# Seven block products for eight in the gate and value projections of the last two token blocks

## The chip, the cores and the metric

The kernel runs on one core of one Trainium2 chip. The metric is the device time of one execution in microseconds (us). The kernel before was timed in three runs; one more execution was profiled.

## The reference, cut to what matters

Attention over chunks of 32 tokens (each chunk sees 8 memory keys and 56 neighbours) gives `x` with 3072 rows of 512. Two feed-forward layers follow:

```python
gate = 1.0 / (1.0 + np.exp(-(x @ w_gate)))      # w_gate, w_val: 512 x 1536
x2 = (gate * (x @ w_val)) @ w_out               # w_out: 1536 x 512
h = x2 @ w_in                                   # w_in: 512 x 2048
P = a[0] + a[1] * h + a[2] * h**2 + a[3] * h**3
Q = 1.0 + np.abs(b[0]) * np.abs(h) + np.abs(b[1]) * h**2
y = (P / (Q + 1e-06)) @ w_out2                  # 2048 x 512
```

## The kernel before

The 3072 tokens are six blocks of 512. Every product of the two layers is three matmuls, since each operand is split into a rounded high part and the rest (`TERMS`: high by high, high by low, low by high). A matmul here multiplies a 128 x 128 weight tile by 512 tokens.

**First layer.** The loop over `steps` has 72 steps: for each block `j` the twelve slices `f` of 128 features. A step computes the gate (`gate_val` with m = 0: 4 slices of K times 3 terms, 12 matmuls), the value (m = 1, 12 more), their product `g` in two parts (`g_split`), and then the output product of the step before (`out1`, 12 matmuls into four accumulators that stay over the block). The weights stay in SBUF as 32-bit words (`wf`), and every step of every block splits its three weight tiles again: ScalarE writes the high part (`w1_hi`, line 323), VectorE the low part (`w1_lo`, line 327).

**Around it.** The attention of block `j` is done in pairs of 128 tokens during the steps of block `j - 1`, in three places of the PE order: scores (`pair_qk`), transposes (`pair_t`) and values (`pair_out`), put into a step by the table `plan`. The weights of the second layer arrive as 64-bit words, are converted (`conv2`), stored in DRAM as `w2d` and read again in block 5 and after, where they are split.

**Second layer.** 96 steps of `h2` (12 matmuls), the rational function on ScalarE and VectorE, and `out2` (12 matmuls) five steps later.

The order on every engine is the order of the code. Each engine runs its own list in that order, and so does SyncE (SP), which issues nearly all the transfers: one that waits for a buffer holds up all those behind it. Buffers come from pools: `w` (32 tiles of 4 KB a partition), `t` for intermediates, and PSUM with four banks `ps` beside the four accumulators.

Of the kernel before, what the change touches and what calls it, by code (L numbers as in the profile page):

```python
# [34 lines left out]
PAD = 840  # L35
# [3 lines left out]
NPAIR = 8  # L39


@with_exitstack
def fused_kernel(ctx: ExitStack, tc: tile.TileContext, q, k, v, w1, w2, coef, x2d, w2d, out):
# [16 lines left out]
    psp = ctx.enter_context(tc.tile_pool(name="ps", bufs=4, space=PSUM))  # L60

# [110 lines left out]
    def attn_pv(t, x, n0):  # L172
# [82 lines left out]
    def pair_pv(t, x, n0):  # L257
# [53 lines left out]
    def unit1(f, m):  # L311
        u = 3 * f + m
        if u % 2 == 0 and u // 2 not in wf:
            wf[u // 2] = wpool.tile([P, 2, 512], F32, tag="w", name=f"wf{u // 2}")
        return wf[u // 2][:, u % 2]

    def load_w1(f):
        for m in range(3):
            load_stage(f"1_{f}_{m}", w1[:, f, m * 512 : (m + 1) * 512])

    def split_hi(key, src):
        wp[key] = wpool.tile([P, 2, 512], F32R, tag="w", name="wp" + "_".join(map(str, key)))
        nc.scalar.activation(out=wp[key][:, 0], in_=src, func=ACTF.Copy)  # L323
# [4 lines left out]


# [3 lines left out]
    xt, gp, sgs = {}, {}, {}  # L333

    def gate_val(j, f, m, c0, n):
        w, x = wp[1, j, f, m], xt[j]
        pt = ps(f"h{j}_{f}_{m}_{c0}")[:, 0:n]
        for kt in range(KT):
            for i, (a, b) in enumerate(TERMS):
                nc.tensor.matmul(  # L340
                    pt,
                    lhsT=w[:, a, kt * P : (kt + 1) * P],
                    rhs=x[:, kt, b, c0 : c0 + n],
                    start=(kt == 0 and i == 0),
                    stop=(kt == KT - 1 and i == 2),
                )
        if m == 0:
            sgs[j, f, c0] = t2(f"sg{j}_{f}_{c0}")[:, 0:n]
            nc.scalar.activation(out=sgs[j, f, c0], in_=pt, func=ACTF.Sigmoid)  # L349
        else:  # L350
            sg = sgs[j, f, c0]
            nc.vector.tensor_tensor(out=sg, in0=sg, in1=pt, op=ALU.mult)  # L352
        if c0 + n == BLOCKS1[j]:
            del wp[1, j, f, m]
# [29 lines left out]

    def store1(j):
        for d in range(KT):
            s = t2(f"x2s{j}_{d}")
            if d % 2 and j < NB1 - 1:
                nc.vector.tensor_copy(s, acc[j][d])
            else:  # L390
                nc.scalar.activation(out=s, in_=acc[j][d], func=ACTF.Copy)
            nc.sync.dma_start(out=x2d[j, :, d], in_=s)
        del acc[j]


    x2f, x2, w2f, rat = {}, {}, {}, {}
# [5 lines left out]
    def split_x2(j, d):  # L402
        if d == 0:
            x2[j] = xpool.tile([P, KT, 2, 512], F32R, tag="x", name=f"x2_{j}")
        s, t = x2f.pop((j, d)), x2[j]
        nc.scalar.activation(out=t[:, d, 0], in_=s, func=ACTF.Copy)
        nc.vector.tensor_tensor(out=t[:, d, 1], in0=s, in1=t[:, d, 0].bitcast(F32), op=ALU.subtract)

    def load_w2(i):
        w2f[i] = t2(f"w2f{i}")  # L410
        nc.sync.dma_start(out=w2f[i], in_=w2d[i])

    def split_w2(i):
        s = w2f.pop(i)
        split_hi((2, i), s)
        split_lo((2, i), s)

    def h2(j, f):
# [3 lines left out]
        for kt in range(KT):  # L422
            for i, (a, b) in enumerate(TERMS):
# [3 lines left out]
                    rhs=x[:, kt, b],  # L427
# [59 lines left out]

    const.tile([P, PAD], F32, name="pad")


    NB1 = len(BLOCKS1)

    def pv(t):
        j, n0 = t // 4, t % 4 * P
        if n0 == 0:
            xt[j] = xpool.tile([P, KT, 2, 512], F32R, tag="x", name=f"x{j}")
        (attn_pv if t < NPAIR else pair_pv)(t, xt[j], n0)

# [294 lines left out]
```

## Time and profile before

| | |
|---|---|
| median of three runs | 1197.31 us (1196.38 to 1197.61) |
| the profiled execution | 1197.76 us; its span, first to last instruction, is 1196.0 us |
| PE (matmul) busy | 1183.2 us, 99% |
| PE weight loads busy | 975.4 us, 82% |
| VectorE (DVE) / ScalarE (ACT) busy | 842.0 us, 70% / 747.2 us, 62% |
| moved by DMA | 101.68 MB, 85 GB/s over the span |
| granted TensorE clock, mean | 0.993 of full speed (2.4 GHz) |

The profiled time is the span and 1.8 us around it. Busy shares are means over stages that have different limits.

### The profile page before, as it was taken

The numbers are of one execution on the slowest core, as the hardware profiler recorded it, in microseconds if no ns is written. First come the engines' busy times: TensorE is split into PE (matmuls) and PEld (weight loads), VectorE is DVE, ScalarE is ACT, GpSimd is POOL, SyncE is SP. The second block draws the span as 40 slices with busy tenths as digits, with TensorE's granted clock in tenths as the row PEclk, the third lists the DMA queues.
The fourth block names the chain that finished last, engine by engine and source line by source line (L and its number), as shares of the span: only waits on it lengthen the run. The fifth ranks groups of instructions, "written<-read, shape, count | busy, mean of one in ns | idle before, by whom it ended". The sixth has DMA issues, their size and how long they took to land.

```text
span 1196.0 us, 19841 instructions
## 1 busy us (share of the span) xinstructions
PE 1183.2 (99%) x8086; PEld 975.4 (82%) x8089; DVE 842.0 (70%) x1312; ACT 747.2 (62%) x1278; POOL 2.1 (0%) x15
## 2 busy tenths in 40 slices
PE   7999999999999999999999999999999999999998
PEld 4788888888888888888888888888888888888887
DVE  5777454555646454654566599898898898888885
ACT  5887445454546454554555687767776767776764
POOL 0000000000000000000000000000000000000000
PEclk8899999999999999999999999999999999999999
DMA  9854042234225224322532110100100100100000
GB/s 380 299 193 132 26 141 89 100 128 140 89 100 170 90 93 139 114 76 98 185 95 63 55 36 10 53 17 1 53 18 1 54 18 10 45 18 1 36 1 35
DMA packets 40123, 101.68 MB, mean 85 GB/s; under 512 B 4576, under 2 KB 4832, under 8 KB 40032
## 3 DMA queue, kind: packets, MB, share of 16 engines
q1 hardware_dynamic: 39456, 99.01, 24.6%
q8 instruction: 63, 1.03, 0.4%
q10 hardware_dynamic: 576, 1.41, 0.3%
q14 instruction: 28, 0.23, 0.1%
HBM read 79.43 MB, written 20.97 MB: 84 GB/s over the span
## 4 chain that ended last, share of the span: by engine, by line
PE 98%; DMA 1%; ACT 1%; issue 0%; DVE 0%; SPq 0%
PE h L340 33%; PE acc L463 22%; PE h L424 22%; PE acc L375 17%; PE xp L268 1%; PE sp L208 1%; PE xp L183 1%; DMA st<-w_in 1%; PE tp L253 1%; DMA q<-q_in 0%; PE tp L168 0%; PE sp L109 0%; ACT st L298 0%; ACT st L299 0%; ACT at L170 0%
## 5 line engine op out<-in xcount | busy, mean ns | idle before, releaser
L340 PE MATMUL h<-x,wp 128*128 128x512 f32 x1728 | 409.9, 392 | 1.5 <-ACT x L192 1.5
L340 PEld LDWEIGHTS h<-x,wp 128*128 128x128 f32 x1728 | 325.2, 189 | 69.2 <-ACT x L192 1.6
L424 PE MATMUL h<-x,wp 128*128 128x512 f32 x1152 | 276.5, 389 | 0.0
L463 PE MATMUL acc<-wp,g 128*128 128x512 f32 x1152 | 275.9, 389 | 0.0
L424 PEld LDWEIGHTS h<-x,wp 128*128 128x128 f32 x1152 | 216.2, 188 | 44.9
L463 PEld LDWEIGHTS acc<-wp,g 128*128 128x128 f32 x1152 | 216.2, 188 | 44.9
L375 PE MATMUL acc<-g,wp 128*128 128x512 f32 x864 | 212.8, 392 | 0.0
L375 PEld LDWEIGHTS acc<-g,wp 128*128 128x128 f32 x864 | 160.6, 188 | 34.0
L352 DVE TENSOR_TENSOR sg<-sg,h 128x512 f32<-128x512 f32 x72 | 49.5, 687 | 159.8 <-PE h L340 109.8
L432 ACT ACTIVATE t<-h,cf 128x512 f32<-128x512 f32 x96 | 74.6, 778 | 131.4 <-PE h L424 131.4
L358 ACT ACTIVATE g<-sg 128x512 fp32r<-128x512 f32 x72 | 45.4, 630 | 166.1 <-DVE sg L352 166.1
L327 DVE TENSOR_TENSOR wp<-wf,wp 128x512 fp32r<-128x512 f32 x216 | 136.6, 685 | 7.6 <-ACT wp L323 7.2
L323 ACT ACTIVATE wp<-wf 128x512 fp32r<-128x512 f32 x216 | 120.7, 621 | 10.2 <-PE h L340 8.8
L435 DVE TENSOR_TENSOR t<-t,h 128x512 f32<-128x512 f32 x96 | 65.8, 686 | 47.8 <-ACT hh L434 46.5
L349 ACT ACTIVATE sg<-h 128x512 f32<-128x512 f32 x72 | 43.0, 597 | 75.0 <-PE h L340 74.3
L359 DVE TENSOR_TENSOR g<-sg,g 128x512 fp32r<-128x512 f32 x72 | 49.9, 693 | 56.1 <-ACT g L358 56.1
L436 DVE SCALAR_TENSOR_TENSOR t<-t,cf,h 128x512 f32<-128x512 f32 x96 | 71.8, 748 | 3.4
L444 ACT ACTIVATE y<-qq,qc 128x512 f32<-128x512 f32 x96 | 70.0, 729 | 3.9 <-DVE qq L437 3.3
L437 DVE SCALAR_TENSOR_TENSOR qq<-hh,cab,qq 128x512 f32<-128x512 f32 x96 | 71.8, 748 | 0.0
L451 DVE SCALAR_TENSOR_TENSOR t<-t,cf,y 128x512 f32<-128x512 f32 x96 | 71.8, 748 | 0.0
L450 DVE SCALAR_TENSOR_TENSOR qq<-qq,y 128x512 f32<-128x512 f32 x96 | 66.0, 687 | 8.1 <-ACT y L445 8.1
L452 DVE SCALAR_TENSOR_TENSOR t<-qq,t 128x512 f32<-128x512 f32 x96 | 66.5, 692 | 3.3
(74 smaller groups left out, 833.2 us busy)
## 6 DMA issues: line engine op xcount, KB each, us to landing
st<-w_in SPq DMA_DIRECT2D x68, 512.0 KB, 4.7
v<-v_in SPq DMA_DIRECT2D x24, 512.0 KB, 4.7
k<-k_in SPq DMA_DIRECT2D x21, 416.0 KB, 4.0
w2d<-c SPq DMA_DIRECT2D x32, 256.0 KB, 2.1
w2f<-w2d SPq DMA_DIRECT2D x32, 256.0 KB, 3.4
q<-q_in SPq DMA_DIRECT2D x24, 256.0 KB, 3.6
x2d<-x2s SPq DMA_DIRECT2D x24, 256.0 KB, 2.8
x2f<-x2d SPq DMA_DIRECT2D x24, 256.0 KB, 3.1
```

The lines of the kernel that those rows point to most:

```text
L323: nc.scalar.activation(out=wp[key][:, 0], in_=src, func=ACTF.Copy)
L327: nc.vector.tensor_tensor(out=t[:, 1], in0=src, in1=t[:, 0].bitcast(F32), op=ALU.subtract)
L340: nc.tensor.matmul(pt, lhsT=w[:, a, kt * P : (kt + 1) * P], rhs=x[:, kt, b, c0 : c0 + n], start=(kt == 0 and i == 0), stop=(kt == KT - 1 a ...
L375: nc.tensor.matmul(acc[j][d][:, c0 : c0 + n], lhsT=w[:, a, d * P : (d + 1) * P], rhs=g[:, b, 0:n], start=(f == 0 and c0 == 0 and i == 0), ...
L424: nc.tensor.matmul(hp, lhsT=w[:, a, kt * P : (kt + 1) * P], rhs=x[:, kt, b], start=(kt == 0 and i == 0), stop=(kt == KT - 1 and i == 2),)
L432: nc.scalar.activation(out=t, in_=hp, func=ACTF.Identity, scale=cf[:, 3:4], bias=cf[:, 2:3])
L436: nc.vector.scalar_tensor_tensor(out=t, in0=t, scalar=cf[:, 1:2], in1=hp, op0=ALU.add, op1=ALU.mult)
L437: nc.vector.scalar_tensor_tensor(out=qq, in0=hh, scalar=cab[:, 1:2], in1=qq, op0=ALU.mult, op1=ALU.add)
L444: nc.scalar.activation(out=y, in_=qq, func=ACTF.Abs_reciprocal_sqrt, bias=qc[:, 0:1])
L451: nc.vector.scalar_tensor_tensor(out=t, in0=t, scalar=cf[:, 0:1], in1=y, op0=ALU.add, op1=ALU.mult)
L452: nc.vector.scalar_tensor_tensor(out=t, in0=qq, scalar=2.0, in1=t, op0=ALU.subtract, op1=ALU.mult)
L463: nc.tensor.matmul(acc[j][m], lhsT=g[:, a, m * P : (m + 1) * P], rhs=w[:, b], start=(f == 0 and i == 0), stop=(f == NF2 - 1 and i == 2),)
```

## The change

Blocks 4 and 5 (`JA`, `JB`) are no longer computed one after the other. Two blocks of tokens, two slices of features and two halves of K make a 2 x 2 x 2 block product, which the new function `quad` computes with seven products in place of eight. A product is 6 matmuls (two slices of K, three terms). `quad(fp, 0, ...)` makes the gates of features 2fp and 2fp + 1 for both blocks, `quad(fp, 1, ...)` the values; there are six `fp`. The seven products use sums and differences of the operands:

- of the weights: `w_comb` forms four per pair of features, one in each step of blocks 1 and 2, and stores them split (`wqs`);
- of x: `x_comb` forms five in steps 43 to 47, from x kept whole (`xf`);
- of the results: five additions in each `quad`.

So x of block 5 must be there before block 4 begins. The attention of blocks 2 to 5 is now done in the steps of blocks 1 to 3, one pair every three steps. A step exists only for blocks 0 to 3 (48 steps); after the last `quad` come 13 visits of `out1` alone.

SBUF would not hold all of this, so split weights are kept in DRAM: gate and value tiles are stored in block 1 and output tiles in block 2 (`wqa`), and blocks 3, 4 and 5 load them split instead of splitting them. The second layer's weights are stored split too. A split tile is 128 x 1024 words, 512 KB. Pools are opened and closed by stage; `w` has 18 buffers, `t` 14. The weight tiles of gate and value are laid out by halves of K, each with gate and value columns.

```diff
-    wpool = ctx.enter_context(tc.tile_pool(name="w", bufs=32))
-    xpool = ctx.enter_context(tc.tile_pool(name="x", bufs=2))
+    wpool = ctx.enter_context(tc.tile_pool(name="w", bufs=18))
+    xpool = ctx.enter_context(tc.tile_pool(name="x", bufs=4))
-    tpool = ctx.enter_context(tc.tile_pool(name="t", bufs=12))
+    tpool = ctx.enter_context(tc.tile_pool(name="t", bufs=14))
...
+    def load_qk2(t):
+        u = qs[t] = wpool.tile([P, 2, 4, P], F32, tag="w", name=f"q{t}")
+        nc.sync.dma_start(out=u, in_=q[t : t + 2].rearrange("t p r n -> p t r n"))
+        for i in range(2):
+            u = ks[t + i] = wpool.tile([P, KW], F32, tag="w", name=f"k{t + i}")
+            nc.sync.dma_start(out=u, in_=k[t + i])
...
+            c = slice(n0, n0 + 2 * P)
+            if j <= JA:
+                hi, lo = (xt[j][h][:, :, b, c] for b in range(2))
+                nc.scalar.activation(out=hi, in_=xps[h], func=ACTF.Copy)
+                nc.vector.tensor_tensor(out=lo, in0=xps[h], in1=hi.bitcast(F32), op=ALU.subtract)
+            if j >= JA:
+                nc.scalar.activation(out=xf[j][:, h, :, c], in_=xps[h], func=ACTF.Copy)
...
+    def store_split(key, dst):
+        nc.sync.dma_start(out=dst, in_=wp[key].bitcast(F32))
...
+    def load_split(key, src, p=None, tag="w"):
+        nc.sync.dma_start(out=split_tile(key, p, tag).bitcast(F32), in_=src)
...
+    def x_comb(o, c):
+        c = slice(256 * c, 256 * c + 256)
+        a, b = xf[JA], xf[JB]
+        key = f"{o}_{c.start}"
+        if o not in xop:
+            xop[o] = b_tile(f"b{o}", F32R, [P, 2, 2, 512])
+        if o == "22":
+            xs[key] = b[:, 1, :, c]
+            return
+        t = xs[key] = t2(f"xs{key}").rearrange("p (k n) -> p k n", k=2)
+        x0, x1 = {
+            "1": (b[:, 0, :, c], a[:, 0, :, c]),
+            "2": (b[:, 1, :, c], xs.get(f"1_{c.start}")),
+            "3": (b[:, 1, :, c], b[:, 0, :, c]),
+            "4": (a[:, 1, :, c], xs.get(f"2_{c.start}")),
+        }[o]
+        nc.vector.tensor_tensor(out=t, in0=x0, in1=x1, op=ALU.subtract)
...
+    def w_comb(i):
+        fp, o = divmod(i, 4)
+        a, b = wf["gv", 2 * fp], wf["gv", 2 * fp + 1]
+        sf[i] = t2(f"sf{i}")
+        x0, x1, op = (
+            lambda: (b[:, 0], b[:, 1], ALU.add),
+            lambda: (sf[i - 1], a[:, 0], ALU.subtract),
+            lambda: (a[:, 0], b[:, 0], ALU.subtract),
+            lambda: (a[:, 1], sf[i - 2], ALU.subtract),
+        )[o]()
+        nc.vector.tensor_tensor(out=sf[i], in0=x0, in1=x1, op=op)
...
+    PRODUCTS = (
+        (("a", 0, 0), "11", 0),
+        (("s", 1), "2", 1),
+        (("s", 0), "1", 2),
+        (("s", 2), "3", 3),
+        (("a", 0, 1), "21", 0),
+        (("s", 3), "22", 2),
+        (("a", 1, 1), "4", 3),
+    )
...
+    def quad(fp, m, fill):
+        f0, f1 = 2 * fp, 2 * fp + 1
+        bank = [ps(f"p{fp}_{m}_{i}") for i in range(4)]
+        def product(i):
+            w, o, n = PRODUCTS[i]
+            wt, x = wp[quad_key(fp, w)], xop[o]
+            for kt in range(2):
+                c = m * 256 + kt * P
+                for t, (a, b) in enumerate(TERMS):
+                    nc.tensor.matmul(
+                        bank[n],
+                        lhsT=wt[:, a, c : c + P],
+                        rhs=x[:, kt, b],
+                        start=(i < 4 and kt == 0 and t == 0),
+                        stop=(kt == 1 and t == 2),
+                        skip_group_check=True,
+                    )
+            if m == 1:
+                del wp[quad_key(fp, w)]
+                if i < len(PRODUCTS) - AHEAD and fp < NF1 // 2 - 1:
+                    quad_load(fp + 1, i + AHEAD, 1)
+        def add(out, x0, x1):
+            nc.vector.tensor_tensor(out=out, in0=x0, in1=x1, op=ALU.add)
+        def done(j, f, c):
+            if m == 0:
+                if c is None:
+                    sgs[j, f] = t2(f"sg{j}_{f}")
+                    nc.scalar.activation(out=sgs[j, f], in_=bank[0], func=ACTF.Sigmoid)
+                else:
+                    sgs[j, f] = c
+                    nc.scalar.activation(out=c, in_=c, func=ACTF.Sigmoid)
+                return
+            sg = sgs.pop((j, f))
+            y = bank[0] if c is None else c
+            if j == JB:
+                nc.vector.tensor_tensor(out=g5(f), in0=sg, in1=y, op=ALU.mult)
+                return
+            nc.vector.tensor_tensor(out=sg, in0=sg, in1=y, op=ALU.mult)
+            g_split((1, j, f), sg, 512)
+        tag = f"{fp}_{m}"
+        product(0)
+        p1 = t2(f"p1_{tag}")
+        nc.scalar.activation(out=p1, in_=bank[0], func=ACTF.Copy)
+        product(1)
+        u = t2(f"u_{tag}")
+        add(u, p1, bank[1])
+        product(2)
+        v = t2(f"v_{tag}")
+        add(v, u, bank[2])
+        product(3)
+        c22 = t2(f"c22_{tag}")
+        add(c22, v, bank[3])
+        done(JB, f1, c22)
+        product(4)
+        done(JA, f0, None)
+        fill()
+        product(5)
+        c12 = t2(f"c12_{tag}")
+        add(c12, u, bank[2])
+        done(JB, f0, c12)
+        product(6)
+        c21 = t2(f"c21_{tag}")
+        add(c21, u, bank[3])
+        done(JA, f1, c21)
...
+    GV, OUT = (0, 1), (2,)
+    for si, (j, f) in enumerate(steps):
+        if j < 3:
+            if si:
+                at(si - 1, w1_hi, j, f, GV)
+                at(si - 1, w1_lo, j, f, GV)
+                at(si, w1_hi, j, f, OUT)
+                at(si, w1_lo, j, f, OUT)
+            if j == 1:
+                at(si, w1_store, j, f, GV)
+            if j == 2:
+                at(si + 1, w1_store, j, f, OUT)
+        else:
+            at(si - 2, w1_load, j, f, GV)
+            at(si - 1, w1_load, j, f, OUT)
...
+    for i in range(2 * NF1):
+        s0 = NF1 + i
+        at(s0, w_comb, i)
+        at(s0, w_comb_hi, i)
+        at(s0, w_comb_lo, i)
+        at(s0 + 1, w_comb_store, i)
...
-    for t in range(NPAIR, NBLK, 2):
-        j, i = divmod(t, 4)
-        s0, s1 = (NF1 * (j - 1) + o for o in ((6, 10) if i else (1, 5)))
-        for u in (t, t + 1):
-            at(s0 - 2, load_qk, u)
-            at(s1 - 3, load_v, u)
+    for i, t in enumerate(range(NPAIR, NBLK, 2)):
+        s0, s1 = ((13, 18), (16, 21), (19, 24), (22, 27), (31, 36), (34, 39), (37, 42), (40, 45))[i]
+        at(s0 - 1, load_qk2, t)
+        at(s1 - 2, load_v, t)
+        at(s1 - 2, load_v, t + 1)
         at(s0, pair_qk, t)
         at(s0, pair_max, t)
...
+        nv = 0
+        for fp in range(NF1 // 2):
+            for m in range(2):
+                i = 2 * fp + m
+                store1_end()
+                if m == 0 and fp < NF1 // 2 - 1:
+                    quad_load(fp + 1, 0, AHEAD)
+                if i:
+                    load_out(1 if fp < NF1 // 2 - 1 else 3)
+                for n in conv_in[i - 3]:
+                    conv2_store(n)
+                for n in conv_in[i]:
+                    conv2_load(n)
+                if fp == NF1 // 2 - 1:
+                    for d in (2 * m, 2 * m + 1):
+                        load_x2(0, d)
+                def fill():
+                    for n in conv_in[i - 2]:
+                        conv2_hi(n)
+                        conv2_lo(n)
+                    for n in conv_in[i - 1]:
+                        conv2(n)
+                quad(fp, m, fill)
+                for n in conv_in[i - 1]:
+                    conv2_bits(n)
+                if fp or m == 0:
+                    out1(*visits[nv])
+                    nv += 1
...
+        for i in range(len(visits) - nv - 1):
+            load_out(1)
+            store1_end()
+            j, f = visits[nv]
+            for nxt in visits[nv + 2 : nv + 3]:
+                if nxt[0] == JB:
+                    g_split((1, *nxt), g5(nxt[1]), 512)
+            if 4 <= i < KT + 4:
+                split_x2(0, i - 4)
+            load_w2(1)
+            if f >= NF1 - 1 - PRE and j == JB:
+                h2(0, f - NF1 + 1 + PRE)
+            out1(j, f)
+            nv += 1
```

What stands in the lists of three engines, before and after. On PE, one slice of features of block 5 before (`h` gate and value, `acc` the output product of the slice before):

```order
L340 MATMUL h_1_0_0_6046<-x_5371,wp_5_1_0_5963 128x512 x12
L340 MATMUL h_1_1_0_6064<-x_5371,wp_5_1_1_5965 128x512 x12
L375 MATMUL acc_0_6081<-g_5_0_0_6001,wp_5_0_2_5912 128x512 x3
L375 MATMUL acc_1_6082<-g_5_0_0_6001,wp_5_0_2_5912 128x512 x3
L375 MATMUL acc_2_6083<-g_5_0_0_6001,wp_5_0_2_5912 128x512 x3
L375 MATMUL acc_3_6084<-g_5_0_0_6001,wp_5_0_2_5912 128x512 x3
```

And in the changed kernel the values of the last pair of features, 10 and 11, for blocks 4 and 5 (`p_1_n` is bank n; `b` and `x` are operands made of x, `wpq` loaded weights), with what follows:

```order
L493 MATMUL p_1_0_6573<-x_0_4318,wpq_a_0_6267 128x512 x6
L493 MATMUL p_1_1_6574<-b_5127,wpq_s_6269 128x512 x6
L493 MATMUL p_1_2_6575<-b_5124,wpq_s_6271 128x512 x6
L493 MATMUL p_1_3_6576<-b_5205,wpq_s_6273 128x512 x6
L493 MATMUL p_1_0_6573<-x_1_4319,wpq_a_1_6381 128x512 x6
L493 MATMUL p_1_2_6575<-b_5266,wpq_s_6391 128x512 x6
L493 MATMUL p_1_3_6576<-b_5202,wpq_a_1_6401 128x512 x6
L577 MATMUL acc_0_5751<-g_4_9_6451,wp_4_9_2_6468 128x512 x3
```

The four values of that pair took 48 matmuls and take 42; banks 0, 2 and 3 are written twice, with reads of them between.

On VectorE, the changed kernel in the same stretch (`g_2` holds block 5's products, `g_4` the split products of block 4, `wpw` a weight of the second layer):

```order
L507 TENSOR_TENSOR u_1_6591<-p_5_1_6583,p_1_1_6574 128x512
L507 TENSOR_TENSOR v_1_6599<-u_1_6591,p_1_2_6575 128x512
L507 TENSOR_TENSOR c_5_1_6607<-v_1_6599,p_1_3_6576 128x512
L521 TENSOR_TENSOR g_2_6413<-c_5_0_6514,c_5_1_6607 128x512
L523 TENSOR_TENSOR sg_10_6523<-sg_10_6523,p_1_0_6573 128x512
L563 TENSOR_TENSOR g_4_10_6617<-sg_10_6523,g_4_10_6617 128x512
L352 TENSOR_TENSOR wpw_31_6620<-c_31_6548,wpw_31_6620 128x512
L507 TENSOR_TENSOR c_5_1_6629<-u_1_6591,p_1_2_6575 128x512
L521 TENSOR_TENSOR g_2_6413<-c_5_0_6536,c_5_1_6629 128x512
L507 TENSOR_TENSOR c_5_1_6638<-u_1_6591,p_1_3_6576 128x512
L523 TENSOR_TENSOR c_5_0_6545<-c_5_0_6545,c_5_1_6638 128x512
L563 TENSOR_TENSOR g_4_11_6641<-c_5_0_6545,g_4_11_6641 128x512
```

Before, a step of block 5 had three weight splits (line 327), one multiplication (352) and one low part (359) here; now it has the additions of line 507, and no weight of the first layer is split.

On SP, the changed kernel from the values of pair 3 on (`wpq_a_1`, `wpq_s`, `wpq_a_1` are the last three weights of pair 4, the next four the first of pair 5, `st` a weight of the second layer to convert):

```order
L358 DMA wpq_a_1_6184<-wqa 128x1024
L358 DMA wpq_s_6194<-wqs 128x1024
L358 DMA wpq_a_1_6204<-wqa 128x1024
L358 DMA wpq_a_0_6267<-wqa 128x1024
L358 DMA wpq_s_6269<-wqs 128x1024
L358 DMA wpq_s_6271<-wqs 128x1024
L358 DMA wpq_s_6273<-wqs 128x1024
L358 DMA wp_4_7_2_6275<-wqa 128x1024
L355 DMA w2d<-wpw_26_6227 128x1024
L310 DMA st_30_6278<-w_in 128x512
```

Before, no weight of the first layer was loaded after block 0; now every pair of features needs nine such tiles.

## Rows read from the trace of the kernel before

**Rows 1.** The page, its first lines: busy us (share of the span) and instructions.

```profile
span 1196.0 us, 19841 instructions
PE 1183.2 (99%) x8086; PEld 975.4 (82%) x8089; DVE 842.0 (70%) x1312; ACT 747.2 (62%) x1278; POOL 2.1 (0%) x15
```

**Rows 2.** Waits of PE, longest of seven: us in total, times, longest.

```profile
PE xp L183 <- issue: 1.8, 1, 1.8
PE xp L183 <- ACT at L170: 1.6, 2, 1.2
PE h L340 <- ACT x L192: 1.5, 1, 1.5
```

**Rows 3.** Chain that ended last, two steps of block 4: start us, us, what.

```profile
602.10 5.44 PE h L340 x24
607.54 2.72 PE acc L375 x12
610.26 5.44 PE h L340 x24
```

**Rows 4.** The same chain where a pair's attention stands.

```profile
153.15 1.36 PE acc L375 x6
...
157.56 5.44 PE h L340 x24
...
176.60 0.87 PE tp L253 x8
...
188.37 1.36 PE acc L375 x6
...
193.32 5.44 PE h L340 x24
```

**Rows 5.** The page's costliest groups: count, busy us, mean ns, idle before.

```profile
L340 PE MATMUL h<-x,wp 128*128 128x512 f32 x1728 | 409.9, 392 | 1.5 <-ACT x L192 1.5
L340 PEld LDWEIGHTS h<-x,wp 128*128 128x128 f32 x1728 | 325.2, 189 | 69.2 <-ACT x L192 1.6
```

**Rows 6.** Groups by line and form, on VectorE and ScalarE.

```profile
L327 DVE TENSOR_TENSOR wp<-wf,wp 128x512 fp32r<-128x512 f32 x216 | 136.6, 685 | 7.6 <-ACT wp L323 7.2
...
L359 DVE TENSOR_TENSOR g<-sg,g 128x512 fp32r<-128x512 f32 x72 | 49.9, 693 | 56.1 <-ACT g L358 56.1
L352 DVE TENSOR_TENSOR sg<-sg,h 128x512 f32<-128x512 f32 x72 | 49.5, 687 | 159.8 <-PE h L340 109.8 <-issue 36.6 <-ACT sg L349 9.8
...
L358 ACT ACTIVATE g<-sg 128x512 fp32r<-128x512 f32 x72 | 45.4, 630 | 166.1 <-DVE sg L352 166.1
...
L304 DVE SCALAR_TENSOR_TENSOR c<-st 128x512 int32<-128x512 int32 x32 | 22.1, 690 | 8.1 <-ACT st L299 7.3 <-DMA k<-k_in 0.8
...
L246 DVE TENSOR_TENSOR s<-s,r 128x1024 f32<-128x1024 f32 x8 | 9.8, 1225 | 0.3
L243 DVE TENSOR_REDUCE r<-s 128x16 f32<-128x1024 f32 x8 | 9.7, 1212 | 0.0
```

**Rows 7.** Windows: stretch, its us, busy by engine, granted PE clock, DMA share, GB/s.

```profile
15.00:20.00 5.00, 2.27 (x80) 1.86 (x66) 4.47 (x13) 4.91 (x10) 0.00 (x0) 0.90 1.03 412
20.00:25.00 5.00, 4.34 (x80) 3.81 (x80) 2.73 (x6) 4.00 (x8) 0.00 (x0) 0.50 1.03 419
...
30.00:35.00 5.00, 4.74 (x11) 3.69 (x12) 3.49 (x7) 5.00 (x11) 0.00 (x0) 0.50 1.03 413
35.00:40.00 5.00, 5.00 (x21) 4.02 (x21) 3.79 (x6) 4.97 (x9) 0.00 (x0) 0.89 1.03 420
5.00:40.00 35.00, 27.35 (x574) 21.61 (x577) 24.81 (x54) 24.34 (x48) 0.20 (x1) 0.76 1.03 415
80.00:100.00 20.00, 20.00 (x212) 16.22 (x211) 14.78 (x28) 15.46 (x32) 0.20 (x1) 1.00 0.61 186
```

**Rows 8.** The page's DMA issues: count, KB each, median us to landing.

```profile
st<-w_in SPq DMA_DIRECT2D x68, 512.0 KB, 4.7
```

**Rows 9.** The view of tile st, its transfers over the whole run.

```profile
DMA to landing us min/median/max: 3.4/4.7/10.0
```

More of the change, by code (lines that the diff above doesn't have):

```diff
@@ L60, in fused_kernel, with open_pool @@
     psp = ctx.enter_context(tc.tile_pool(name="ps", bufs=4, space=PSUM))
+    lower, upper = ExitStack(), ExitStack()
+    ctx.enter_context(lower)
+    ctx.enter_context(upper)
+    pool = {}
+    def open_pool(where, name, bufs):
+        pool[name] = where.enter_context(tc.tile_pool(name=name, bufs=bufs, reuse_waits="tile"))
+    open_pool(lower, "f1", 4)
+    open_pool(upper, "f2", 14)
     ident = const.tile([P, P], F32, name="ident")
@@ L341, in gate_val, with gv_out @@
                     pt,
[L342 to L345, printed above, removed]
+                    lhsT=w[:, a, c : c + P],
+                    rhs=x[:, kt, b],
+                    start=(h == 0 and kt == 0 and i == 0),
+                    stop=(h == 1 and kt == 1 and i == 2),
                 )
+    def gv_out(pt, j, f, m):
         if m == 0:
-            sgs[j, f, c0] = t2(f"sg{j}_{f}_{c0}")[:, 0:n]
@@ L356, in g_split, with g5 @@
+    g5s = {}
+    def g5(f):
+        if f // 4 not in g5s:
+            p, tag = (xpool, "x") if f < 4 else (pool["g5"], "g5")
+            g5s[f // 4] = p.tile([P, 4, 512], F32, tag=tag, name=f"g5_{f // 4}")
+        return g5s[f // 4][:, f % 4]
     def g_split(key, sg, n):
@@ L383, in out1 @@
             store1(j)
+    held = []
     def store1(j):
@@ L387, in store1, with store1_end @@
             s = t2(f"x2s{j}_{d}")
[L388 to L391, printed above, removed]
+            nc.scalar.activation(out=s, in_=acc[j][d], func=ACTF.Copy)
+            held.append((j, d, s))
+        del acc[j]
+    def store1_end():
+        for j, d, s in held:
             nc.sync.dma_start(out=x2d[j, :, d], in_=s)
-        del acc[j]
-    x2f, x2, w2f, rat = {}, {}, {}, {}
+        held.clear()
+    x2f, x2, rat = {}, {}, {}
     def load_x2(j, d):
@@ L403, in split_x2 @@
         if d == 0:
[L404 to L416, printed above, removed]
+            x2[j] = [x_tile(f"x2_{j}_{h}") for h in range(2)]
+        s, t = x2f.pop((j, d)), x2[j][d // 2][:, d % 2]
+        nc.scalar.activation(out=t[:, 0], in_=s, func=ACTF.Copy)
+        nc.vector.tensor_tensor(out=t[:, 1], in0=s, in1=t[:, 0].bitcast(F32), op=ALU.subtract)
     def h2(j, f):
@@ L494, in pv @@
         j, n0 = t // 4, t % 4 * P
-        if n0 == 0:
-            xt[j] = xpool.tile([P, KT, 2, 512], F32R, tag="x", name=f"x{j}")
-        (attn_pv if t < NPAIR else pair_pv)(t, xt[j], n0)
+        if n0 == 0 and j <= JA:
+            xt[j] = [x_tile(f"x{j}_{h}") for h in range(2)]
+            if j == JA:
+                xop["11"], xop["21"] = xt[j]
+        if n0 == 0 and j >= JA:
+            xf[j] = b_tile(f"xf{j}", F32, [P, 2, 2, 512])
+        if t < NPAIR:
+            attn_pv(t, xt[j], n0)
+        else:
+            pair_pv(t, j, n0)
     def pair_out(t):
@@ L665, in fused_kernel @@
         conv_scale("1_2_1")
-        for si, (j, f, c0, n) in enumerate(steps):
+        for si, (j, f) in enumerate(steps):
             acts = plan.get(si, [])
+            if si == 3 * NF1:
+                upper.close()
+                lower.close()
+                open_pool(lower, "g5", 2)
+                open_pool(upper, "b", 7)
             def run(*fns):
@@ new lines, in fused_kernel, with load_w2 @@
+        for n in conv_in[9]:
+            conv2_store(n)
+        nc.scalar.activation(out=cab, in_=cf[:, 4:6], func=ACTF.Abs)
+        upper.close()
+        open_pool(upper, "c", 14)
+        need = sorted(range(2 * NF2), key=lambda u: u // 2 + LAG2 * (u % 2))
+        w2_next = 0
+        def load_w2(n):
+            nonlocal w2_next
+            for u in need[w2_next : w2_next + n]:
+                late_pool = w2_next >= 14
+                load_split((2, u), w2d[u], *((wpool, "w") if late_pool else (pool["c"], "c")))
+                w2_next += 1
@@ L713, in fused_kernel @@
                 if si == PRE:
-                    out1(*steps[-1])
+                    out1(*visits[-1])
             if si >= LAG2:
```

267 lines of the change are left out of this document (164 added, 103 removed).

## The prediction, made before the result was known

> **What bounds the kernel now.** I read the page's busy times first: the matmuls of PE are busy in 1183.2 of 1196.0 us [rows 1]. A busy share alone doesn't show that a matmul less is time less, so I read who PE waited for: its longest wait is 1.8 us, and all those of [rows 2] fall into the launch, the first 30 us. Then the chain that ended last, in order of time [rows 3]: a step of block 4 is 24 matmuls of gate and value in 5.44 us and 12 of the output product in 2.72 us, and the next step begins where it ends, after 8.16 us. So a matmul of 512 columns costs 5.44 / 24 = 0.2267 us (the mean of 392 ns in [rows 5] counts what overlaps). Nothing stands between the steps there, in blocks 4 and 5 no more than elsewhere. PE's list is the bound in the very stage that changes; what leaves it leaves the time, unless PE begins to wait.
>
> **What is removed from PE.** Blocks 4 and 5 have 2 x 12 x 24 = 576 matmuls of gate and value before, and 6 x 2 x 7 x 6 = 504 after; the order on PE shows 42 rows' worth where 48 stood. 72 matmuls by 0.2267 us are 16.3 us. Attention is moved and not changed: a pair costs PE 1.69 us of scores (153.15 to 157.56, less 2.72), 0.87 us of transposes and 2.23 us of values (188.37 to 193.32, less 2.72) [rows 4], 4.8 us in blocks 1 to 3 as elsewhere.
>
> By the Trainium skill (Perfetto Trace Analysis, Identifying the Most-Contended Engine), the busy share of matmuls is no good measure of PE's headroom, and that of the weight loads is better. By that the removed work would be 72 loads of 189 ns [rows 5], 13.6 us. The trace is against it: the loads are busy 82% [rows 1] while matmuls follow each other without a gap.
>
> **What is added, and what hides it.**
>
> VectorE in blocks 1 and 2, one step of the dense stretch (steps 16 to 24): three low parts and that of `w_comb`, 4 x 0.685; the sum itself, bounded by the same row, 0.685; the gate's product 0.687; the low part of g 0.693 [rows 6]. That is 4.8 us. The second layer's weights come 5 in 8 steps at 0.690 + 0.685, 0.86 us a step. A pair of attention every three steps costs a reduction 1.212, a product 1.225, two maxima, two subtractions and two low parts of x near 0.69 each and 0.4 of small ones, 7.0 us, 2.3 a step. Together 8.0 us, and about 0.8 more in which VectorE stands for ScalarE's high part of g (56.1 us in 72 times, [rows 6]). A step takes 8.16 + 4.8 / 3 = 9.8 us. VectorE is near 90% and PE doesn't need its results at once: g is read a whole step later, the weights in the next one. I take 0; if the cover were gone, the excess over 9.8 us would come once a step.
>
> VectorE in a `quad` of values: 5 additions, 4 products, 2 low parts of g and up to 2 low parts and 2 conversions of second-layer weights, 15 x 0.69 = 10.4 us, and twice 0.77 us of standing for ScalarE, 11.9 us. PE takes 42 x 0.2267 + 2.72 = 12.2 us there, and the `quad` of gates after it has only half of that work. Within a `quad` the tightest reads are those between two writes of a bank: `v` must have read bank 2 before the sixth product begins. It does so at 4.08 + 0.69 = 4.8 us, and that product begins at 6.8 us; bank 3 likewise, 6.1 against 8.2 us. The tightest place of all is the end of the last `quad`: the low part of feature 11 of block 4 is done at about 13.8 us from its start (the twelve rows of the order, one after the other), and PE wants it after 42 + 12 + 12 matmuls, at 15.0 us. Slack 1.2 us. I take 0.5 us for this place and others like it; a further operation of 0.7 us in each of the six would be 4.2 us.
>
> ScalarE has less to do: 1207 instructions where 1255 stood.
>
> Transfers. From step 12 to the last visit of `out1` the order of SP has 300 of them, 149.6 MB, in 36 x 8.16 + 8 x 4.8 + 504 x 0.2267 + 24 x 2.72 + 3 x 2.72 = 519.8 us: 288 GB/s, where the whole span had 85. Block 3 is the worst: 35.2 MB in 112.9 us, 312 GB/s, since it loads 36 weight tiles while the last pairs of attention load their own. Bounds of what the queues can move: the launch moved 415 GB/s over 35 us at a share of 1.03; 80 to 100 us had 186 GB/s at a share of 0.61, which is 305 at 1 [rows 7]. At 415 block 3 needs 85 us; at 305 it needs 115.4, and PE would wait 2.5 us. The tiles here have rows of 4 KB, as the `st` loads that fill the launch, so I take 415 and no wait. A price for stores of 4 KB rows is not in the trace; they are in the 305 only in part.
>
> When must a load have landed? Weights of products 5 to 7 of the next pair are issued last, when products 1 to 3 of the values have let their buffers go. From there PE has 36 + 12 + 24 = 72 matmuls until it reads them, 16.3 us (13.6 in the first pair, which has no `out1` there). A load of the same size lands in 4.7 us, median, and 10.0 at most, in the full queue of the launch [rows 8, 9]. The transfers queued behind a waiting one on SP are mostly those of the pair after, with a whole pair of `quad`s, 24 us, to go. For a pair of attention the loads are issued about 3 us into the step before, behind the stores, and read 12 us later.
>
> The launch is the same list. Only the wait of 1.5 us on x [rows 2] may go, since x now lies in two tiles by halves; I count nothing.
>
> **Sum.** 1196.0 - 16.3 + 0.5 = 1180.2 us of span, and 1.8 us around it: 1182.0 us for the profiled execution, which stood 0.45 us above the median. For the median: 1197.3 - 16.3 + 0.5 = 1181.5 us. A difference under 0.2%, 2.4 us, can't be told from no change here.
>
> **Rivals.**
>
> *The weight loads set the pace*: 72 x 0.189 = 13.6 us are saved, 1183.7 + 0.5 = 1184.2 us. Against it stand the gapless matmuls. Chance 0.04.
>
> *VectorE becomes the bound of the values.* If its operations follow each other 10% slower than counted (waits between engines that the sum leaves out), a `quad` of values takes 13.1 us where PE takes 12.2, but the gates' `quad` takes up the lag. It shows only where results are wanted at once, in the last `quad` and in the dense steps: 0.9 us in each of six pairs and 1 us in each of four dense pairs would be 9.4 us, 1190.9 us. For it: VectorE at 90%. Against it: between 80 and 100 us VectorE was busy in 14.78 of 20 us, ScalarE in 15.46, and PE in all 20 [rows 7]. Chance 0.10.
>
> *Slower than before: late weights halve the clock.* If SP is held up, a weight arrives after its 16.3 us and PE stands. In the launch PE stood for 2.7 us between 15 and 20 us; then its granted clock was at half, 1.2 GHz, until after 35 us [rows 7]. Fifteen us at half are 7.5 us of matmuls lost, 10.2 with the stop. One such stop costs 10.2 us: 1191.7 us. Two are 20.4, more than the gain: 1201.9 us. What decides is the rate of the queues: at 149.6 MB / (519.8 + 16.3 us) = 279 GB/s the loads alone eat the gain, and stops come at every pair. Against it: 305 is the lowest bound above, and 16.3 us is above the longest landing of 10.0. Chance 0.06 for two or more stops, 0.04 for one.
>
> *The change doesn't do what it says*: excluded on PE by the count of matmuls.
>
> **How the numbers follow.** My forecast, 1180 to 1184 us with PE waiting for nothing that counts, has 0.76. With the first rival and half of the second, and block 3's 2.5 us and the 4.2 us of six late `quad`s as upper bounds, the range reaches to 1181.5 + 2.5 + 4.2 = 1188.2, and down to 1181.5 - 0.5 - 1.5 = 1179.5 us, if the launch's wait goes and none comes. What lies above is 0.05 of the second rival, 0.04 and 0.06 of the third, and some of the forecast's own error. Faster by over 0.2% (under 1194.9 us): 0.76 + 0.04 + 0.10 + 0.04 less a little for what I haven't seen, 0.91. Within 0.2%: 0.03. Slower: 0.06.
>
> **What would show each step.** In the trace of the changed kernel the seven products should take 42 x 0.2267 = 9.52 us with no idle PE before them; the waits of PE should name nothing above 1 us after the launch; the DMA share in steps 36 to 47 should be near 312 / 415 x 1.03 = 0.77 and below 0.9; VectorE near 90% in the dense steps. Wrong would be: waits of PE on `wpq` by DMA, a granted clock of 0.5 anywhere after 40 us, or waits of `acc` on g by VectorE.

## The result and the profile after

The changed kernel takes 1181.67 us (median of four runs, 1181.36 to 1181.89) where the kernel before took 1197.21 on the same chip: 15.5 us less, a ratio of 0.9871 (95% interval 0.9854 to 0.9888). That is faster by more than the 2.4 us that can be told from no change, 0.2 us from the 1181.5 us forecast and inside its range. The profiled execution took 1181.89 us.

The first lines of its page, against [rows 1]:

```profile
span 1180.1 us, 19991 instructions
PE 1166.8 (99%) x8014; PEld 961.7 (81%) x8017; DVE 846.4 (72%) x1316; ACT 720.5 (61%) x1230; POOL 2.1 (0%) x15
...
DMA packets 63325, 203.42 MB, mean 172 GB/s; under 512 B 7040, under 2 KB 7296, under 8 KB 63232
```

PE has 72 instructions and 16.4 us less, the transfers have doubled, and PE is still busy 99%. Whom it waited for, against [rows 2] (us in total, times, longest):

```profile
PE sp L122 <- DMA k<-k_in: 2.4, 3, 1.1
PE xp L196 <- issue: 2.0, 1, 2.0
PE xp L196 <- ACT at L183: 1.6, 2, 1.3
PE h L376 <- ACT x L205: 1.5, 1, 1.5
```

All of it lies in the launch. The chain that ended last, against [rows 3] (start us, us, what; `p` are the products of a `quad`):

```profile
30.92 13.59 PE h L376 x48
44.51 2.72 PE acc L577 x12
...
567.21 9.52 PE p L493 x42
576.73 2.72 PE acc L577 x12
579.45 9.52 PE p L493 x42
...
1160.17 16.33 PE acc L659 x72
```

And the same places of the kernel before:

```profile
30.26 13.91 PE h L340 x48
44.18 2.72 PE acc L375 x12
...
1176.02 16.33 PE acc L463 x72
```

From the first output product to the last 72 matmuls it was 1131.84 us and is 1115.66: 16.18 us less. That is the gain of the changed stages. The launch ends 0.33 us later here (44.51 for 44.18), but this place moves from execution to execution: in the twelve profiles of the changed kernel and its edits the first output product starts between 43.6 and 45.1 us, in the two with the launch of before at 43.98 (e1) and 44.18. So the 0.33 can't be told from nothing.

Windows of the changed kernel (columns as in [rows 7]): the launch, the dense steps, block 3, the quads.

```profile
20.00:30.00 10.00, 8.24 (x206) 7.43 (x206) 5.47 (x12) 7.07 (x17) 0.00 (x0) 0.50 1.02 407
185.00:275.00 90.00, 90.00 (x1010) 74.72 (x1010) 68.32 (x106) 60.51 (x102) 0.19 (x1) 1.00 0.81 289
361.00:472.00 111.00, 111.00 (x1217) 92.05 (x1217) 50.70 (x76) 49.64 (x82) 0.15 (x1) 1.00 0.89 337
472.00:616.00 144.00, 144.00 (x637) 119.26 (x636) 78.92 (x121) 50.20 (x87) 0.00 (x0) 1.00 0.75 271
```

Behind the launch PE is busy all the time at full clock. VectorE is busy 76% in the dense steps, not 90%, and the transfers of block 3 have a share of 0.89, not 0.77.

### The profile page after: what moved, and what is told of

Its sections match the earlier page's. It is cut to its first block, busy times and chain, and to the rows that moved or that the text cites. A ratio compares the mean times of both kernels' runs of the same rounds, so it can differ in the third digit from the quotient of the medians.

```text
span 1180.1 us, 19991 instructions
## 1 busy us (share of the span) xinstructions
PE 1166.8 (99%) x8014; PEld 961.7 (81%) x8017; DVE 846.4 (72%) x1316; ACT 720.5 (61%) x1230; POOL 2.1 (0%) x15
## 3 DMA queue, kind: packets, MB, share of 16 engines
q8 instruction: 63, 1.03, 0.3%
## 4 chain that ended last, share of the span: by engine, by line
PE 98%; DMA 1%; ACT 1%; issue 0%; DVE 0%; SPq 0%
PE h L376 22%; PE acc L659 22%; PE h L620 22%; PE acc L577 17%; PE p L493 10%; PE xp L289 1%; PE sp L229 1%; PE xp L196 1%; DMA st<-w_in 1%; PE tp L274 1%; DMA q<-q_in 0%; PE tp L181 0%; PE sp L122 0%; ACT st L319 0%; ACT st L320 0%
## 5 line engine op out<-in xcount | busy, mean ns | idle before, releaser
L376 PE MATMUL h<-x,wp 128*128 128x512 f32 x1152 | 275.4, 393 | 1.5 <-ACT x L205 1.5
L620 PE MATMUL h<-x,wp 128*128 128x512 f32 x1152 | 276.5, 389 | 0.0
L376 PEld LDWEIGHTS h<-x,wp 128*128 128x128 f32 x1152 | 216.9, 189 | 46.8 <-ACT x L205 1.6
L620 PEld LDWEIGHTS h<-x,wp 128*128 128x128 f32 x1152 | 216.3, 188 | 44.9
L562 ACT ACTIVATE g<-sg 128x512 fp32r<-128x512 f32 x54 | 34.1, 631 | 131.1 <-DVE sg L390 97.8
L390 DVE TENSOR_TENSOR sg<-sg,h 128x512 f32<-128x512 f32 x48 | 33.0, 687 | 79.5 <-PE h L376 66.7
L493 PE MATMUL p<-b,wpq_s 128*128 128x512 f32 x288 | 69.2, 389 | 0.0
L563 DVE TENSOR_TENSOR g<-sg,g 128x512 fp32r<-128x512 f32 x54 | 37.4, 693 | 43.8 <-ACT g L562 43.8
L563 DVE TENSOR_TENSOR g<-t,g 128x512 fp32r<-128x512 f32 x96 | 65.7, 684 | 0.2 <-ACT g L562 0.2
L629 ACT ACTIVATE qq<-h,cab 128x512 f32<-128x512 f32 x96 | 65.3, 680 | 0.0
```

The lines of the kernel that those rows point to most:

```text
L376: nc.tensor.matmul(pt, lhsT=w[:, a, c : c + P], rhs=x[:, kt, b], start=(h == 0 and kt == 0 and i == 0), stop=(h == 1 and kt == 1 and i == 2),)
L493: nc.tensor.matmul(bank[n], lhsT=wt[:, a, c : c + P], rhs=x[:, kt, b], start=(i < 4 and kt == 0 and t == 0), stop=(kt == 1 and t == 2), sk ...
L563: nc.vector.tensor_tensor(out=t[:, 1, 0:n], in0=sg, in1=t[:, 0, 0:n].bitcast(F32), op=ALU.subtract)
L620: nc.tensor.matmul(hp, lhsT=w[:, a, kt * P : (kt + 1) * P], rhs=x[kt // 2][:, kt % 2, b], start=(kt == 0 and i == 0), stop=(kt == KT - 1 a ...
```

## The experiments

Theory: 72 matmuls of 0.2267 us are the whole gain, and each addition is hidden with some room. The rivals are those of the prediction. Every experiment but the first edits the changed kernel. Each was timed beside the kernel before, and its loss is what its gain over that falls short of 15.5 us; between kernels with no wait of PE such a figure differs by up to 0.7 us.

**The matmuls alone (e1), and what paces them (e2).** In `gate_val` of the kernel before:

```diff
         for kt in range(KT):
+            if j >= 4 and m == 1 and kt == 2:
+                continue
```

> The kernel before, with one of the four slices of K left out of the values of blocks 4 and 5 (so that part of the result is missing): 72 matmuls fewer, nothing added or moved. Theory: the time of a matmul is all there is, 72 x 0.2267 = 16.3 us, so 1197.2 - 16.3 = 1180.9 us, and the changed kernel with all that it adds (1181.7) stands within 1 us of it. Rival, the weight loads pace: 72 x 0.189 = 13.6 us, 1183.6 us. Rival, the additions of the change cost something and the moved work pays for it: this kernel would be faster than 1180 or slower than 1183 us.

Measured: 1181.1 us (1180.85 to 1181.41), where before took 1196.95 beside it: 15.9 us less, against 15.5 for the change. Its chain:

```profile
43.98 2.72 PE acc L377 x12
...
1159.64 16.33 PE acc L465 x72
```

1115.66 us between the two, as in the changed kernel. So all that the change adds and moves costs PE nothing behind the launch.

In `product` of the changed kernel, over the same two slices of K and three terms as the product behind it:

```diff
+            if i == 0:
...
+                        nc.tensor.matmul(
+                            bank[n][:, 0:256],
+                            lhsT=wt[:, a, c : c + P],
+                            rhs=x[:, kt, b, 0:256],
```

> The changed kernel with six more matmuls ahead of the first product of each quad, on the same weights and the same bank, but on 256 columns in place of 512; the product overwrites them. 72 matmuls and 72 weight loads more, half the columns. Theory, the columns pace: 72 x 0.1134 = 8.2 us, 1189.8 us. Rival, the weight loads pace: 72 x 0.189 = 13.6 us, 1195.3 us. Between them would be a limit that neither names.

Measured: 1190.64 us (1189.94 to 1193.76; before 1196.95). The times spread: in the profiled execution (1192.02 us) the last transfer landed in 4.0 us, in that of the changed kernel in 2.0. So the chain decides:

```profile
559.28 0.71 PE p L494 x6
559.99 9.55 PE p L505 x42
```

A `quad` is longer by 0.71 + 0.03 us, twelve of them by 8.9. Six matmuls of half the columns take 0.71 us where six of 512 take 1.36: a load and its matmul follow the pair before every 0.12 us, though a load lasts 0.19. Columns pace, loads don't. The 0.06 us a `quad` above the theory's 0.68 stay unexplained.

**VectorE in the dense steps (e3, e8).** Three more additions a step in `w_comb` (in e8 two):

```diff
+        if 4 <= i <= 12:
+            for _ in range(3):
+                nc.vector.tensor_tensor(out=sf[i], in0=a[:, 0], in1=b[:, 0], op=ALU.add)
```

> The changed kernel with three more additions of 128 x 512 on VectorE in each of the steps 16 to 24 (the dense ones), written to the tile that the step's combination of weights then overwrites. The trace of the changed kernel has VectorE busy 76% there, and operations that follow each other start 0.605 us apart although each lasts 0.69. Theory, VectorE's load is hidden and 90% was too high: 0.76 x 9.8 + 3 x 0.605 = 9.3 us a step, under 9.8, and PE waits for nothing: 1181.7 to 1183 us. Rival of the prediction, VectorE near its bound: 8.0 + 0.8 + 3 x 0.69 = 10.9 us a step, 1.1 over, in 9 steps 9.7 us: 1191 us.

> As the run with three more additions in each of the steps 16 to 24, but with two. There the additions, which write one tile one after the other, started 0.725 us apart and cost 6.9 us in nine steps. Theory: VectorE is busy 7.4 of the 9.8 us of a step and stands 0.7 to 0.8 for ScalarE's high part of g; 8.2 + 3 x 0.725 = 10.4 is over 9.8, 8.2 + 2 x 0.725 = 9.6 is under it: 1181.7 to 1182.7 us. Rival, every addition costs its share: 2/3 of 6.9 us, 1186.3 us.

Measured: three cost 7.2 us (1188.62, 1187.26 to 1189.83; before 1196.95), two 1.2 (1182.39, 1182.17 to 1182.97; before 1196.69), of which PE's waits in that stretch are 0.5. With three, PE waits 5.1 us in that stretch for VectorE and for ScalarE behind it:

```profile
PE tp L274 <- DVE s L257: 1.8, 1, 1.8
PE h L376 <- ACT sg L387: 1.4, 1, 1.4
PE tp L274 <- ACT s L245: 1.2, 1, 1.2
PE h L376 <- DVE s L257: 0.7, 1, 0.7
```

and its window, what VectorE itself waits for there most, and the twelve matmuls behind the last two waits of PE (from its chain) are

```profile
185.00:275.00 90.00, 84.95 (x974) 69.46 (x973) 77.64 (x118) 53.59 (x92) 0.19 (x1) 0.98 0.71 249
```

```profile
DVE g L566 <- ACT g L565: 5.6, 8, 0.7
DVE x L301 <- ACT x L300: 3.6, 3, 1.9
```

```profile
252.43 4.37 PE h L376 x12
```

These twelve matmuls take 2.72 us at full clock. Here the clock fell (0.58 granted from 252 to 256 us), which cost 1.65 us more. The mean clock of the four executions fits: 0.991 in the two at 1189.6 and 1189.8 us, 0.993 and 0.994 in those at 1187.7 and 1187.3.

With two:

```profile
185.00:275.00 90.00, 89.50 (x1005) 73.75 (x1005) 76.76 (x120) 58.63 (x100) 0.20 (x1) 1.00 0.78 269
```

VectorE goes from 76% to 85% with two and only to 86% with three. That is its limit in this stretch: with three its waits come to 12.3 us (5.6 and 3.6 for ScalarE, 3.1 for masks that POOL writes), and with the 77.64 us of work they fill the 90. The expectation of e3, no cost, was wrong: it left this standing out, and it counted 0.605 us for additions that start 0.725 apart. The room is two additions a step, 1.45 us, at a price of about 1 us over nine steps.

**The turn of a bank in the values (e4, e9).** Six more additions in a `quad` of values (in e9 three):

```diff
         v = t2(f"v_{tag}")
+        if m == 1:
+            for _ in range(6):
+                add(v, u, p1)
```

> The changed kernel with six more additions on VectorE in each quad of values, ahead of the one that reads bank 2. Theory, a bank's turn is what limits there: in the trace of the changed kernel that read ends 4.8 us after the quad's start and the sixth product begins at 6.8; six more by 0.605 make it 8.4 to 8.9, so PE waits 1.6 to 2.1 us once in each of six quads, 10 to 13 us: 1191.5 to 1194.5 us, with the granted clock at 1.00. Rival, each stop also halves the clock as the one in the launch did, with 7.5 us more a stop: some 55 us, about 1235 us. Rival, the slack is larger than I read: no change.

> As the run with six more additions in each quad of values, but with three. Theory, the slack at bank 2 is the 2.0 us that the trace shows: the read of bank 2 would end 4.8 + 3 x 0.725 = 7.0 us after the quad's start at the earliest 6.8 wanted, 0.2 us late in each of six quads: 1181.7 to 1183 us. Rival, every addition costs its share of what six cost: 8 us, 1190 us.

Measured: six cost 16.8 us (1198.18, 1195.75 to 1199.11; before 1196.95), three 0.6 (1181.76, 1181.28 to 1182.26; before 1196.69), with no wait of PE behind the launch. PE's waits with six, and two of its six stops in the chain:

```profile
PE p L493 <- DVE v L507: 11.5, 6, 1.9
```

```profile
567.88 0.70 DVE v L507
568.60 0.70 DVE v L507
...
569.40 0.70 DVE v L507
...
570.14 4.61 PE p L493 x12
...
598.43 3.03 PE p L493 x12
```

The bank is the limit and its slack is the 2.0 us that the order gave. Twelve matmuls take 2.72 us without a stop; behind two of the six stops they took 4.61, as the clock fell (0.76 granted from 568 to 573 us, 1.00 from 543 to 548 behind another stop), and 3.0 behind the other four. 11.5 + 2 x 1.9 + 4 x 0.3 = 16.5 us. The 0.3 doesn't hang on the length of the stop: in e8 twelve matmuls behind a stop of 0.2 us took 3.00 us too. What it consists of stays open. The stops are as the theory had them, 10 to 13 us, but the time is above its 1194.5 us, since it took the clock to stay at 1.00. Nor does the same stop always cost the clock: in six of the ten executions (1198.1 to 1199.1 us) the mean clock was 0.990 or 0.991, in the other four (1195.8 to 1196.5 us) 0.993.

**The queues (e5, e6).** More stores of 512 KB: behind `run(w1_load, quad_load)` of each step of block 3 (e5, two as shown, or one), and ahead of each `quad` (e6):

```diff
+            if j == 3:
+                for n in range(2):
+                    nc.sync.dma_start(out=xd[2 * f + n], in_=xt[3][0][:, 0].bitcast(F32))
...
+                for n in range(2):
+                    nc.sync.dma_start(out=xd[2 * i + n], in_=xop["11"][:, 0].bitcast(F32))
```

> The changed kernel with one more store of 512 KB in each of the twelve steps of block 3 (a part of x of block 3 to a scratch place that nobody reads, waiting for nothing): 35.2 + 6.3 = 41.5 MB in 112.9 us, 367 GB/s. The trace of the changed kernel has 294 GB/s at a share of 0.78 in 377 to 488 us, which is 377 at 1. Theory, the queues have room (377 to 415 GB/s): no wait of PE, 1181.7 to 1183 us. Rival, the lower bound of the prediction (305 GB/s): 136 us for 112.9, some 20 us late, 1200 us or more.

> The same with two stores in each step: 47.8 MB, 423 GB/s, above all that the traces show. Theory: the limit is passed; at 415 GB/s block 3 takes 115 us, 2 us late, at 377 it takes 127 us, 14 us late, and PE waits for split weights by DMA: 1184 to 1197 us. Rival, stores and loads don't share one limit: no change.

> The changed kernel with two more stores of 512 KB ahead of each of the twelve quads (a part of x of block 4 to a scratch place that nobody reads): 273 + 88 = 361 GB/s over the quads. Theory: the room of a pair of quads, 24 us, and of the 16.3 us between issue and use hide it, with at most one or two short waits: 1181.7 to 1185 us. Rival, at 305 GB/s the quads would take 170 us for 144, 26 us late: 1208 us.

Measured beside a before of 1197.01: one 1182.16 us (1181.09 to 1183.65; PE waits 0.5 us, once), two 1185.42 (1184.41 to 1186.02), in the quads 1181.82 (1181.33 to 1182.66). With two a step, PE's waits outside the launch, and block 3:

```profile
PE h L376 <- DMA wp<-wqa: 2.6, 3, 1.7
```

```profile
377.00:472.00 95.00, 92.45 (x952) 75.88 (x940) 41.40 (x62) 39.78 (x64) 0.15 (x1) 1.00 1.03 413
```

The queues carry 413 GB/s of loads and stores for 95 us at a share of 1.03, what they carried in the launch [rows 7]; the 305 is excluded. Three stops of 1.7 us at most left the clock at 1.00 in the profiled execution (mean 0.994); of the other three, one has a mean of 0.991. In the quads two more stores a `quad` make

```profile
520.00:570.00 50.00, 50.00 (x223) 41.39 (x222) 28.17 (x44) 18.16 (x32) 0.00 (x0) 1.00 0.97 377
```

and PE doesn't wait.

**A late weight (e7, e10).** The store stands in e10 alone:

```diff
-                    quad_load(fp + 1, 0, AHEAD)
+                    quad_load(fp + 1, int(fp == 2), AHEAD - int(fp == 2))
...
                 quad(fp, m, fill)
+                if fp == 2 and m == 1:
+                    nc.sync.dma_start(out=xd[0][:, 0], in_=g5(4))
+                    quad_load(3, 0, 1)
```

> The changed kernel with one load moved: the weights of the first product of the fourth pair of features are issued ahead of the output product that comes just before it, 2.7 us before PE wants them, and not a pair of quads earlier. Landing 6 to 8 us, so one stop of PE of 3 to 6 us. Rival of the prediction as it was priced: the stop halves the granted clock for 15 us, 7.5 us more, 1192 to 1195 us in all. Theory after the stops of 1.9 us, of which the clock fell in two of six and gave 1.6 us away each time: a longer stop lets it fall for certain, but only for some 3 to 4 us, so 5 to 8 us in all, 1187 to 1190 us.

Measured: 1181.28 us (1180.95 to 1181.74; before 1197.01), and no stop. SP's timeline (start us, us) tells why:

```profile
531.71 3.04 SPq L358 DMA_DIRECT2D wpq_a<-wqa  x3
```

The moved load is among these three, at least 7.8 us ahead of its product at 542.56. SP doesn't follow PE: it goes down its own list as buffers come free. The expectation's 2.7 us took a place in the code for a time.

> The changed kernel with one load made late for certain: the weights of the first product of the fourth pair of features are issued behind a store (256 KB to a scratch place) of a value that the quad before finishes 1.3 us after its end. PE wants the weights 2.7 us after that end, they land 5 to 7 us after their issue: one stop of 3.5 to 5.5 us. Rival of the prediction as it was priced: the granted clock is at half for 15 us behind it, 7.5 us more, 1193 to 1195 us. Theory: the clock falls, but for 3 to 4 us as behind two of the six stops of 1.9 us, so 1.6 to 2 us more: 1187 to 1189 us. Third: it doesn't fall at all, as with the stops of up to 1.7 us in block 3: 1185 to 1187 us.

Measured: 1188.48 us (1187.74 to 1189.45; before 1196.69), 7.3 us lost. Its wait, chain and windows:

```profile
PE p L493 <- DMA wpq_a<-wqa: 4.0, 1, 4.0
```

```profile
542.03 4.91 DMA wpq_a<-wqa
546.95 0.04 issue
546.99 12.13 PE p L493 x42
```

```profile
540.00:545.00 5.00, 2.98 (x14) 2.12 (x12) 4.23 (x8) 2.31 (x5) 0.00 (x0) 1.00 0.56 151
545.00:550.00 5.00, 3.01 (x7) 2.43 (x8) 0.50 (x1) 0.04 (x1) 0.00 (x0) 0.51 0.98 368
550.00:555.00 5.00, 5.00 (x19) 3.98 (x19) 1.38 (x2) 0.55 (x1) 0.00 (x0) 0.81 0.97 363
555.00:560.00 5.00, 5.00 (x24) 4.14 (x23) 3.10 (x6) 3.89 (x7) 0.00 (x0) 1.00 0.52 188
```

A stop of 4.0 us, then the clock near half (0.51; half is 1.2 GHz), then full again: the seven products take 12.13 us for 9.52, so 2.6 us more, not 7.5.

**The launch (e11).** Ahead of the values of the first 128 tokens:

```diff
         attn_t(1)
+        idle_mm(6)
         conv_scale("1_0_2")
```

> The changed kernel with six more idle matmuls on PE in the launch, between the transposes of the second pair and the values of the first, where PE waits 1.3 us for ScalarE. Theory: the stop there and the one of 2.0 us behind it let the clock fall from about 20 to 38 us; if the first is filled and the clock stays, PE gains at most 5 us there (the waits for ScalarE's parts of x and the weights stay): 1177 to 1181 us. Rival: the stop behind it alone lets the clock fall, or ScalarE and the loads set the start of the first step anyway: 1181.4 to 1182.2 us.

Measured: 1181.85 us (1181.52 to 1182.38; before 1196.69), no gain. The wait for ScalarE shrinks from 1.6 to 0.2 us, and yet:

```profile
10.00:20.00 10.00, 7.20 (x169) 4.45 (x156) 9.24 (x26) 5.44 (x11) 0.00 (x0) 1.00 1.03 402
20.00:30.00 10.00, 7.82 (x212) 7.03 (x212) 5.41 (x12) 6.86 (x17) 0.00 (x0) 0.61 1.02 406
```

The clock falls a little later (0.61 for 0.50 from 20 to 30 us), and the first `h` still waits 1.5 us for ScalarE's x and starts at 30.89 us for 30.92. The stop of 2.1 us behind the filled one stands, so the rival fits; which of its two halves holds was not told apart. No run here beat the changed kernel by more than the spread of its times.

## Why the prediction was right, point by point

- **PE's list is the bound, 72 x 0.2267 = 16.3 us.** Right: 16.18 by the chains, and the same 1115.66 us with the matmuls simply left out. That the time came within 0.2 us of the forecast is luck on top: executions of the changed kernel differ by 0.5 us, and the 0.5 us allowed for a late place were not lost there.
- **The weight loads as the measure.** It fails, as the prediction held. 72 loads more, of 190 ns each, cost 8.9 us with half the columns and not 13.6. The Trainium skill (Perfetto Trace Analysis, Identifying the Most-Contended Engine) judges PE's headroom by MFU (the share of the peak rate reached) and the busy share of weight loads. The trace is against the second: it stands at 81% where no matmul can be added without its price.
- **0.5 us at the end of the last `quad`.** Nothing was lost there. The low part of feature 11 of block 4 was done at 617.49 us, 13.6 after the `quad`'s start at 603.93 (forecast 13.8, wanted at 15.0), and cost nothing. VectorE's timeline there (the line of `v` is its read of bank 2):

```profile
608.05 0.69 DVE L507 TENSOR_TENSOR v<-u,p 128x512 f32<-128x512 f32 x1 [0.60 <-PE p L493]
...
612.76 0.69 DVE L352 TENSOR_TENSOR wpw<-c,wpw 128x512 fp32r<-128x512 f32 x1
613.36 0.68 DVE L507 TENSOR_TENSOR c<-u,p 128x512 f32<-128x512 f32 x1
...
616.80 0.69 DVE L563 TENSOR_TENSOR g<-c,g 128x512 fp32r<-128x512 f32 x1 [0.70 <-ACT g L562]
```

  In the launch the first `h` does start later, at 30.5 to 31.1 us in the twelve profiles of the changed kernel and its edits, at 30.17 and 30.26 with that of before. The queues carried 407 GB/s there and 416 before (20 to 30 us). But by the first output product the difference is lost in the spread (43.6 to 45.1 against 43.98 and 44.18 us), and what makes the first `h` later stays open.
- **VectorE near 90% in the dense steps, price 0.** The price was right, both parts of the share mis-sized. Of the 90%, 0.8 us of 9.8 were standing, so the busy share forecast was 8.0 / 9.8 = 82%, and 76% was measured: I had added durations, and independent operations of 0.69 us start 0.60 apart (612.76 and 613.36 above). The standing was 1.6 us a step and not 0.8, since more than the high part of g is waited for (changed kernel, 185 to 275 us, with 4.0 us more for POOL):

```profile
DVE g L563 <- ACT g L562: 6.5, 9, 0.8
DVE x L301 <- ACT x L300: 4.0, 3, 1.9
```

  The two errors offset each other, so the 90% named the room about rightly by luck: at 85 to 86% busy PE waits (e3, e8). The rival was nearer than 76% shows: 1.45 us more a step cost about 1 us in all, 2.2 us cost 7.
- **VectorE in a `quad` of values, 11.9 of 12.2 us.** Too high. In five of the six it was busy 7.3 us in 12.24 us of PE, with 11 or 12 operations where the sum had 15 at their full durations. So VectorE as the bound of the values, the second rival, stood farther off than the sum had it.
- **The turn of the banks.** Right to 0.1 us. Bank 2's read ended at 608.74, 4.8 us after the start of the last `quad`, as forecast; three additions fit into the slack of 2.0 us, six don't.
- **The queues: 415 GB/s and no wait.** Right (413 in e5). The share of block 3 was mis-sized, 0.89 for 0.77, just under the 0.9 that I had set. More was moved in it than its own list has, 337 GB/s for 312, which by the prediction's rate makes 0.84. The rest is the rate: 337 at 0.89 is 379 GB/s at a share of 1, not 415, and the dense steps' 289 at 0.81 is 357. The Trainium skill (DMA: Bandwidth & Descriptors, Where 436 GB/s comes from) has some 358 GB/s as what binds between HBM and SBUF and 435 as the ceiling of the ports. One core works here: e5's 413 lies above the first, and the trace agrees with the second.
- **Late weights.** None was late. The mechanism is real (e10), but its price was mis-sized: 6.6 us, not 10.2. The stop was longer than the 2.7 us priced (4.0), the slow clock behind it cost 2.6 us and not 7.5: the launch, from which the price came and where PE stops again and again, was no measure for a single stop. The view of the tile of `wqs` weights has

```profile
DMA to landing us min/median/max: 4.6/6.3/11.0
```

  against the 16.3 us between issue and use (forecast: 4.7 median, 10.0 at most).
- **The wait of 1.5 us on x may go.** It stayed.

## What to carry to other kernels

Where matmuls follow each other without a gap, price a removed one by the interval in the chain, and check it by leaving the matmuls out of the old kernel (part of its result is then missing). That gives the gain without the additions, and the difference to the real change is what these cost. Measure room by adding work until the bound engine waits; a busy share of 76% had nine points of room here, not 24, while queues at 0.89 took one more store a step with a single wait of 0.5 us. And to make a transfer late, tie it to a result: its place in the code doesn't, because the issuing engine runs ahead.

## What the runs showed of the hardware

- VectorE starts operations of 0.69 us 0.60 us apart where they don't depend on each other, and 0.72 apart where they write one tile in turn (e4, 567.88 and 568.60).
- A stop of PE doesn't always take the clock. In the profiled executions three of up to 1.7 us took nothing (e5), two of six of 1.9 us gave 1.9 us away each (e4), one of 1.8 and one of 0.7 us close together gave 1.65 (e3), one of 4.0 us gave 2.6 (e10). Other executions of e3, e4 and e5 show other mean clocks, so the same stop may or may not cost it. Filling one of the launch's stops moved the long stretch at half there little (e11); what keeps it so long stays open.
- A VectorE that waits for other engines in every step is full below 100%: 86% busy and 14% waiting (e3).
